# A fused attention and two-expert-layer kernel: one written order of all engines up to the third batch, and elementwise work moved off GpSimd

## Chip, cores and metric

One core of a Trainium2 chip. The metric is device time in microseconds (us), the median over runs of the same kernel. Engines are called TensorE (PE; its weight loads PEld), VectorE (DVE), ScalarE (ACT), GpSimd (POOL) and SyncE (SP), which issues most of the transfers.

## What is computed

Three layers follow each other. The inputs are arrays of 64-bit floats for the second layer's weights and of 32-bit floats elsewhere.

1. Attention on 4 batches of 8 heads, 768 positions, 64 wide. Each row sees the keys within 16 positions, and 24 summary keys: the maxima of K over blocks of 32 rows, with the means of V over the same blocks as their values.
2. A dense layer without a nonlinearity except a product, on 3072 rows: `a = x @ w1`, `b = x @ w2`, `x2 = ((a * b) @ w3) @ w_out`, with 512, 1024, 1024 and 512 columns.
3. A layer of 8 experts: rows whose score `x2 @ w_skip` is positive go to the expert with the largest of 8 logits, through `relu(x @ w1[e]) @ w2[e]`, scaled by the softmax weight and added to the row; other rows pass unchanged.

```python
k_sum = k.reshape(B, H, nb, block, D).max(axis=3)
v_sum = v.reshape(B, H, nb, block, D).mean(axis=3)
a = np.exp(scores_all)            # near keys and summaries, maximum subtracted
x = np.matmul(a / (np.sum(a, axis=-1, keepdims=True) + 1e-09), v_all)
h = (x @ w1) * (x @ w2) @ w3
x2 = h @ w_out
```

## The kernel before

**Two-part numbers.** The large products use a 32-bit format that TensorE takes at full rate, with each operand split in a high part and the remainder (the low part); a product is three matmuls, high by high, high by low and low by high. `split` (L410) does it: ScalarE copies the high part, VectorE (or an engine passed as `eng`) subtracts it.

**Narrowing.** The second layer's weights come as 64-bit floats, in 40 blocks of 128 by 512 (512 KB each). `Doubles.load` fetches a block to a raw tile, `scaled` makes two passes of ScalarE (L390, L391), and `narrow` three of VectorE: a clip (L400), the lower bits (L401), the sign (L404). Raw tiles come from a ring of 3 and 2 (`NRAW`, `XRAW`) while the fold runs, narrowed ones from a ring of 2 and 3 (`NNT`, `XNT`).

**Fold.** w3 and w_out are multiplied once into one matrix `wh`, `wl` (with the gate's columns in front: 522 columns in parts of 266 and 256), so that a row block needs a*b and one product `x2`.

**Attention** works on 16 pairs of heads (4 batches of 4). For a pair, K and Q are transposed (one PSUM tile, `tr`); then, for each third of the pair, letters name the steps: `S` the scores, `a` the masked minimum on VectorE (L196) and the exponential on ScalarE (L206), `b` the normalisation (L218 to L224), `T` and `t` the transposition and its copy, `V` and `v` the product with V and its copy. `m` loads half of the rows for the sums of V to the tile `vt`, of which there is one (`VTB = 1`), and `r` sums them (L134; with `pool` in four adds on GpSimd, L131 and L132). The loads of the next V tiles take the sums.

**Dense layer.** A row block is 256 rows; there are 12. Slabs (128 by 1024 in 32 bits; 7, then 12) hold attention's output, its two parts, and the two parts of each half of a*b. `ab` makes one of 8 chunks in 24 matmuls (L557), `ab_out` takes it from PSUM: a copy (L574), the product (L575), the high part (L576) and on GpSimd the low part (L577). `x2` makes the 96 matmuls of a block (L591) in 8 pieces of 12. The first four chunks of blocks 0 to 2 run as soon as half of w1 and w2 is there.

**Order.** Two strings (`PLAN`) give the order of the steps, a letter each, on all five engines, through the fold and the rest of the weights. After them only TensorE's order is written (`manual_schedule(engines={PE})`), by a generator (`AttentionOrder.plan`, `advance`) that puts attention steps between the pieces of the dense blocks; the other engines' instructions are placed by the framework. In the strings GpSimd has nine normalisations and three sums in the first, one of each in the second, and the low halves of the weights (14 in the first). The last batch's three blocks overlap with the splitting of the first expert's weights, and the experts run after them.

Of the kernel before, what the change touches and what calls it, by code (L numbers as in the profile page):

```python
# [7 lines left out]
F32 = mybir.dt.float32  # L8
# [52 lines left out]
STEPS = 11  # L61


class Attention:
# [60 lines left out]
    def sum(self, i, pool=False):  # L125
# [33 lines left out]
    def K_max(self, u):  # L159
        nc, f = self.nc, self.t.pop(("kn", "t"))  # L160
# [9 lines left out]
    def Q_out(self, u, act=False):  # L170
# [4 lines left out]
        if act:  # L175
# [40 lines left out]
    def S_norm(self, u, g, eng=None):  # L216
# [3 lines left out]
        if eng == "act":  # L220
            for i in range(4):
                nc.scalar.activation(pr[:, i, :], pr[:, i, :], AF.Copy, scale=st[:, 2, i : i + 1])
        else:
# [42 lines left out]
class AttentionOrder:  # L266


    KINDS = {
# [3 lines left out]
    }  # L273

    def __init__(self, att, pairs):
        self.att, self.pairs = att, pairs
        self.at = {c: 0 for c in self.KINDS}

    def step(self, c, eng=None):
        a, n = self.att, self.at[c]  # L280
        self.at[c] += 1
        if c == "k":
            a.load(n, "kn")
        elif c == "n":
            a.load(n, "qn")
        elif c == "w":
            a.load_v(n)
        elif c == "m":
            a.load_sum(n)
        elif c == "r":  # L290
            a.sum(n, eng == "pool")
        elif c == "j":
            a.Q_out(n, eng == "act")
        elif c in "KhHQ":
            {"K": a.K, "h": a.K_out, "H": a.K_max, "Q": a.Q}[c](n)
        elif c == "b":
            a.S_norm(*divmod(n, 3), eng)
        else:
            f = {"S": a.S, "a": a.S_exp, "T": a.T, "t": a.T_out, "V": a.V, "v": a.V_out}
            f[c](*divmod(n, 3))  # L300

    def upto(self, c, n):
        end = 4 * B if c in "mr" else self.pairs * self.KINDS[c]
        while self.at[c] < min(n, end):
            self.step(c)

    def plan(self):

        n, out = self.pairs, []
        out += [[("kKhH", 0)], [("nQj", 0)], [("kn", 1)]]  # L310
        for u in range(n):
            last = u + 1 == n
            head = [("kn", u + 2)] if u + 2 < n else []


            i = u + 4
            due = 8 <= i < 4 * B
            head += [("m", i)] if due else []
            out += [
                head + [("Sab", 3 * u)],  # L320
                [("Vv", 3 * u - 1)] if u else [],
                [("Sab", 3 * u + 1)],
                [("Tt", 3 * u)] + ([("r", i)] if due else []),
                [] if last else [("kK", u + 1)],
                [("Sab", 3 * u + 2)] + ([] if last else [("hH", u + 1), ("w", u + 1)]),
                [("Vv", 3 * u)],
                [] if last else [("nQj", u + 1)],
                [("Tt", 3 * u + 1)],
                [("Vv", 3 * u + 1)],
                [("Tt", 3 * u + 2)] + ([("Vv", 3 * u + 2)] if last else []),  # L330
            ]
        return out

    def run(self, todo):
        for cs, n in todo:
            for c in cs:
                self.upto(c, n + 1)
# [8 lines left out]
NRAW, XRAW = 3, 2  # L346
NS0, NS1 = 7, 12
NNT, XNT = 2, 3
WPOS = (6, 8, 9, 11, 12, 13, 14, 15)
PLAN = (  # L350
    (
        "fffAApOpfOAqskfomAssqRUAKuofpfUhsOfAHufpAoOUmpAspnAurffosOmUqQRocsuOAJXfUAopkpmuSUxsOuoS"
        "OaUKASfoabrUuXuznxXhwaATFfpFHFxetzAfFpXTQxfVeJtFXAvpFpAfASFaFpkXfxVfeAeSfXxvaspKFSTFzhna"
        "FHtzFTVXwfApQpffAekxtzevVfJpFnSxsFAvapTztfXFxeASwAappKVAFeSfXspfvAFTXxzkFFhaHptFexVAXzev"
        "fATtQJqfpTsFVFAwtvxpXdVTXxtfvFSFSeAAapxFfefsAzKaSaAmppFFeXVxFTshvRqteFXVxFvdFybeFe"
    ),
    (
        "fzABkpfATtBgsHgqVTBnvfByfmAsgtpBAgBVsfqgBffAsgvpByAgsqgAsfQBrgBABpgpmJngBrdsgSmRSK"
    ),
)  # L360


OTHER = {"z": ("b", "pool"), "Z": ("b", "act"), "R": ("r", "pool"), "J": ("j", "act")}


class Doubles:
# [29 lines left out]
    def narrow(self, raw, t):  # L396
        nc = self.nc
        h, l = raw[:, :, 1], raw[:, :, 0]
        tf = t.bitcast(F32)
        nc.vector.tensor_scalar(tf, tf, HIGH, -HIGH, ALU.min, ALU.max)  # L400
        nc.vector.scalar_tensor_tensor(  # L401
            out=t, in0=t, scalar=3, in1=l, op0=ALU.logical_shift_left, op1=ALU.bitwise_or
        )
        nc.vector.scalar_tensor_tensor(  # L404
            out=t, in0=h, scalar=-0x80000000, in1=t, op0=ALU.bitwise_and, op1=ALU.bitwise_or
        )
        return tf
# [115 lines left out]
class Dense:  # L523
    def __init__(self, tc, pool, slabs, halves, wh, wl, ps):
# [3 lines left out]
        self.xT, self.g = {}, {}  # L528
        self.spare = 2

    def has(self, b, k):
        return (b, k) in self.xT or len(self.slabs.free) > self.spare
# [33 lines left out]
    def ab_out(self, blk, f, pp):  # L566
        nc = self.nc
        if f % 4 == 0:
            if f:
                self.spare = 0  # L570
            self.g[blk, f // 4] = [self.slabs.take(F32R) for _ in range(2)]
        gh, gl = self.g[blk, f // 4]
        a = self.pool.tile([P, BT], F32, tag="a", name="a", bufs=2)
        nc.scalar.activation(a, pp[:, 0, :], AF.Copy)  # L574
        nc.vector.tensor_mul(a, a, pp[:, 1, :])  # L575
# [3 lines left out]
    def x2(self, blk, pool, out, x2e, route, finish):  # L579
        nc, i = self.nc, 2 * blk  # L580
        nf = FF // P
# [645 lines left out]
```

## Time and profile before

| what | value |
|---|---|
| median of 3 runs | 909.35 us (908.76 to 909.97) |
| the profiled execution's own time | 915.21 us |
| its span, first to last instruction | 913.3 us |
| mean granted TensorE clock | 0.968 |
| busy: PE, PEld, DVE, ACT, POOL | 830.8, 772.7, 478.9, 466.2, 223.9 us |
| moved by DMA | 105.02 MB |

Times count from the span's start. Matmuls are pipelined and their ends are modelled, so a busy TensorE need not be at its peak. The clock is granted at two levels, 1 (2.4 GHz) and 0.5; a stretch's value is the mean. In a view of stretches a row gives the stretch, its length, the busy time of PE, PEld, DVE, ACT and POOL with the number of instructions, the granted clock, the mean busy share of the 16 DMA engines and GB/s. In a view of lines a row gives line, engine, operation, output<-inputs, sizes and count, then busy us in all and mean ns of one, then the idle time of the engine just before them and what ended it. In a timeline a row gives start, duration, engine, line, operation, and in brackets the idle time before it with what ended it. L12 is line 12 of the kernel before.

### The profile page before, as it was taken

To read this page: it belongs to the slowest core of one execution; us is meant where nothing else is said; L and a number is where in the kernel's file an instruction comes from. 1 tells how busy PE (TensorE), PEld (TensorE's weight loads), DVE (VectorE), ACT (ScalarE), POOL (GpSimd) and SP (SyncE) were. 2 spreads that over 40 slices of the span, in tenths; PEclk is the share of its full clock that TensorE was granted. 3 is DMA by queue.
4 is the path that set the end of the run, shared out by engine and by line. 5 is a ranking of instruction groups with operands and counts; after the bars stand their busy time and mean duration, and the time that the engine had idled before them with its cause. 6 is when DMAs were issued, how large, how long until landed. Compare 5 with 4: busy or idle time off the path is not lost. (4 is left out here: it accounts for less than half of the span.)

```text
span 913.3 us, 17560 instructions
## 1 busy us (share of the span) xinstructions
PE 830.8 (91%) x6478; PEld 772.7 (85%) x6478; DVE 478.9 (52%) x1496; ACT 466.2 (51%) x1236; POOL 223.9 (25%) x278
## 2 busy tenths in 40 slices
PE   3779999968869999999999999999999979996996
PEld 3669888967769999999999999999998867874785
DVE  5869978845463545353535343522245466254862
ACT  5669986724435654544544544432244355243751
POOL 4312224531102121222121211222243112022231
PEclk9989999998898999999999999999999989997999
DMA  8587944442432433142232020421135456244830
GB/s 240 152 217 200 232 145 129 128 109 85 119 82 84 113 68 89 28 113 49 67 67 78 14 66 2 140 92 47 48 116 193 153 166 218 69 132 132 291 106 22
DMA packets 124612, 105.02 MB, mean 115 GB/s; under 512 B 92914, under 2 KB 98082, under 8 KB 124496
## 3 DMA queue, kind: packets, MB, share of 16 engines
q1 hardware_dynamic: 120144, 98.04, 37.5%
q0 software_dynamic: 4352, 5.51, 2.0%
q8 instruction: 64, 1.05, 0.5%
q14 instruction: 52, 0.43, 0.2%
HBM read 90.45 MB, written 16.64 MB: 117 GB/s over the span
## 5 line engine op out<-in xcount | busy, mean ns | idle before, releaser
L591 PE MATMUL x2p<-wh,slab 128*128 128x266 f32 (+1 forms) x768 | 158.7, 295 | 0.7 <-POOL slab L577 0.6
L591 PEld LDWEIGHTS x2p<-wh,slab 128*128 128x128 f32 x768 | 126.4, 193 | 2.4 <-POOL slab L577 1.0
L577 POOL TENSOR_TENSOR slab<-a,slab 128x256 fp32r<-128x256 f32 x96 | 73.8, 768 | 206.3 <-ACT slab L576 206.1
L591 PE MATMUL x2p<-wl,slab 128*128 128x256 f32 (+1 forms) x384 | 110.4, 287 | 0.0
L575 DVE TENSOR_TENSOR a<-a,ab 128x256 f32<-128x256 f32 x96 | 40.0, 417 | 123.8 <-ACT a L574 123.6
L206 ACT ACTIVATE pr<-pr,st 128x120 f32<-128x120 f32 x192 | 73.2, 384 | 50.2 <-DVE st L196 50.0
L574 ACT ACTIVATE a<-ab 128x256 f32<-128x256 f32 x96 | 36.5, 381 | 95.3 <-PE ab L557 94.1
L557 PE MATMUL ab<-slab,wB1h 128*128 128x256 f32 x384 | 75.6, 294 | 7.9 <-DVE a L575 6.1
L591 PEld LDWEIGHTS x2p<-wl,slab 128*128 128x128 f32 x384 | 74.5, 194 | 0.0
L557 PE MATMUL ab<-slab,wB2h 128*128 128x256 f32 x384 | 74.0, 291 | 0.0
L557 PE MATMUL ab<-slab,wA2h 128*128 128x256 f32 x384 | 72.0, 285 | 0.0
L557 PE MATMUL ab<-slab,wA1h 128*128 128x256 f32 x384 | 72.0, 285 | 0.0
L557 PEld LDWEIGHTS ab<-slab,wB1h 128*128 128x128 f32 x384 | 61.3, 197 | 9.1 <-DVE a L575 6.6
L576 ACT ACTIVATE slab<-a 128x256 fp32r<-128x256 f32 x96 | 40.0, 417 | 55.2 <-DVE a L575 55.0
L557 PEld LDWEIGHTS ab<-slab,wB2h 128*128 128x128 f32 x384 | 60.5, 194 | 0.5
L196 DVE CUSTOM_DVE_ANT_0 pr<-sp,cst 128x120 f32<-128x120 f32 x192 | 42.5, 277 | 34.3 <-PE sp L184 33.3
L557 PEld LDWEIGHTS ab<-slab,wA1h 128*128 128x128 f32 x384 | 58.9, 189 | 0.3
L557 PEld LDWEIGHTS ab<-slab,wA2h 128*128 128x128 f32 x384 | 58.9, 189 | 0.1
L877 POOL DMA_INDIRECT out<-eo,idx x15 | 19.5, 1299 | 149.9 <-DVE eo L874 96.8
L557 PE MATMUL ab<-slab,wB1l 128*128 128x256 f32 x192 | 55.3, 288 | 0.0
L184 PE MATMUL sp<-kaug,qblk 128*128 128x120 f32 x384 | 51.6, 278 | 3.4 <-DVE st L196 3.4
L557 PE MATMUL ab<-slab,wB2l 128*128 128x256 f32 x192 | 54.5, 284 | 0.0
(182 smaller groups left out, 2184.7 us busy)
## 6 DMA issues: line engine op xcount, KB each, us to landing
eraw<-in_moe_w SPq DMA_DIRECT2D x64, 512.0 KB, 5.1
raw<-in_moe_w SPq DMA_DIRECT2D x32, 512.0 KB, 5.2
vaug<-in_v SPq DMA_DIRECT2D x32, 240.0 KB, 5.4
x2e<-row SPq DMA_DIRECT2D x24, 256.5 KB, 2.9
kn<-in_k SPq DMA_DIRECT2D x32, 192.0 KB, 3.1
vt<-in_v SPq DMA_DIRECT2D x16, 384.0 KB
qn<-in_q SPq DMA_DIRECT2D x32, 192.0 KB, 3.0
out<-row SPq DMA_DIRECT2D x24, 256.0 KB
```

The costliest lines, as they stand in the source:

```text
L184: self.nc.tensor.matmul(sp[:, i, 0:KA], self.qblk[:, t, :, :], self.kaug[:, t, :], start=True, stop=True)
L196: nc.vector.tensor_tensor_reduce(out=pr[:, i, :], in0=sp[:, i, 0:KA], in1=self.cst[:, m : m + KA], scale=1.0, scalar=3.0e38, op0=ALU.add, ...
L206: nc.scalar.activation(pr[:, i, :], pr[:, i, :], AF.Exp, scale=-1.0, bias=st[:, 0, i : i + 1], accum_out=st[:, 1, i : i + 1],)
L557: self.nc.tensor.matmul(pp[:, s, :], l[:, c, fs], r[:, c, :], start=(c == 0 and j == 0), stop=(c == 3 and j == 2),)
L574: nc.scalar.activation(a, pp[:, 0, :], AF.Copy)
L575: nc.vector.tensor_mul(a, a, pp[:, 1, :])
L576: nc.scalar.activation(gh[:, f % 4, :], a, AF.Copy)
L577: nc.gpsimd.tensor_sub(gl[:, f % 4, :], a, gh[:, f % 4, :].bitcast(F32))
L591: nc.tensor.matmul(po[:, 0:n], l[:, f % 4, s * P : s * P + P], r[:, f, lo:hi], start=(f == 0 and j == 0), stop=(f == nf - 1 and j == 2),)
L877: nc.gpsimd.indirect_dma_start(out=self.out, out_offset=bass.IndirectOffsetOnAxis(ap=col, axis=0), in_=o, in_offset=None, bounds_check=N - ...
```

## The change

One written order of all five engines now goes on to the end of the third batch's blocks: three strings take the place of two strings and the generator, with new letters for pieces of `x2` (`E`), its copies (`G`) and the router's second part (`N`). Narrowing is three steps with letters of their own (`p`, `i`, `d`). The sums, normalisations and low halves that GpSimd had go to VectorE; the sum is four adds there and no longer a reduction. For blocks 0 to 2 the first half of a*b is kept as one slab and split later (`gsplit`, letter `l`). Raw tiles are 3 and 1 while the fold runs, narrowed tiles 2 and 1; slabs 8, then 12. For the first 8 pairs both halves of Q are copied by ScalarE.

```diff
-NRAW, XRAW = 3, 2
-NS0, NS1 = 7, 12
-NNT, XNT = 2, 3
-WPOS = (6, 8, 9, 11, 12, 13, 14, 15)
+NRAW, XRAW = 3, 1
+NNT, XNT = 2, 1
+NS0, NS1 = 8, 12
+HALVES = 3
+JOBS = "oooooooottttttttwttwttwttwttwwwwwwwwwwww"
...
-        if pool:
-            for n in (8, 4, 2):
-                nc.gpsimd.tensor_add(vt[:, 0:n, :], vt[:, 0:n, :], vt[:, n : 2 * n, :])
-            nc.gpsimd.tensor_add(sm, vt[:, 0, :], vt[:, 1, :])
-        else:
-            nc.vector.tensor_reduce(
-                out=sm, in_=vt.rearrange("r j d -> r d j"), axis=AX.X, op=ALU.add
-            )
+        for n in (8, 4, 2):
+            nc.vector.tensor_add(vt[:, 0:n, :], vt[:, 0:n, :], vt[:, n : 2 * n, :])
+        nc.vector.tensor_add(sm, vt[:, 0, :], vt[:, 1, :])
...
-            (nc.gpsimd if eng == "pool" else nc.vector).tensor_mul(
-                pr, pr, st[:, 2, :].unsqueeze(2).to_broadcast([P, 4, KA])
-            )
+        nc.vector.tensor_mul(pr, pr, st[:, 2, :].unsqueeze(2).to_broadcast([P, 4, KA]))
...
-    def narrow(self, raw, t):
+    def clip(self, t):
...
+    def lower(self, raw, t):
...
+    def signed(self, raw, t):
...
-def split(nc, hi, lo, src, eng=None):
+def split(nc, hi, lo, src):
     nc.scalar.activation(hi, src, AF.Copy)
-    (eng or nc.vector).tensor_sub(lo, src, hi.bitcast(F32))
+    nc.vector.tensor_sub(lo, src, hi.bitcast(F32))
...
+    def ab_out(self, blk, f, pp, whole=False):
+        nc, h = self.nc, f // 4
         a = self.pool.tile([P, BT], F32, tag="a", name="a", bufs=2)
         nc.scalar.activation(a, pp[:, 0, :], AF.Copy)
+        if whole:
+            if f % 4 == 0:
+                self.whole[blk, h] = self.slabs.take(F32)
+            nc.vector.tensor_mul(self.whole[blk, h][:, f % 4, :], a, pp[:, 1, :])
+            return
...
         nc.scalar.activation(gh[:, f % 4, :], a, AF.Copy)
-        nc.gpsimd.tensor_sub(gl[:, f % 4, :], a, gh[:, f % 4, :].bitcast(F32))
+        nc.vector.tensor_sub(gl[:, f % 4, :], a, gh[:, f % 4, :].bitcast(F32))
+
+    def gsplit(self, blk, h):
+        self.g[blk, h] = [self.slabs.take(F32R) for _ in range(2)]
+        w = self.whole.pop((blk, h))
+        split(self.nc, *self.g[blk, h], w)
+        self.slabs.give(w)
...
             nar_s.close()
             att.more = nar_s.enter_context(sb("more", "right"))
+            for c in PLAN[2]:
+                op(c)
             order.__exit__(None, None, None)
             order = tc.manual_schedule(engines={PE})
             order.__enter__()
```

The three strings have 428, 174 and 507 letters. The third begins as follows (`B` a chunk of a*b, `g` its way out of PSUM, `k`, `n`, `w` the loads of K, Q and V, `y` the split of a block of attention's output):

```
hgBHEQgyTEatBjmEVvnbTBGrgtSKVgvaBTEkSgtwbBVaGbETvlSEtnaVETEgHvNGtEVhQGEvbjTkSyEbBgBBgBgmGrtmBEgE
...
```

`K_max` still copies K's maxima on GpSimd (L165), and the router its running counts (L656).

## Rows read from the trace of the kernel before

**Rows 1.** Busy time of each engine by stage, and in the first stage's densest part.

```profile
8.00:144.50 136.50, 110.94 (x896) 103.26 (x895) 112.12 (x264) 105.01 (x273) 37.65 (x39) 0.95 0.76 197
...
184.00:280.00 96.00, 73.76 (x587) 70.41 (x586) 49.06 (x195) 36.19 (x125) 17.97 (x29) 0.88 0.37 100
280.00:587.00 307.00, 305.39 (x2859) 298.37 (x2858) 134.73 (x661) 151.90 (x493) 60.68 (x88) 1.00 0.25 64
...
90.00:105.00 15.00, 13.61 (x125) 13.01 (x124) 14.44 (x37) 13.83 (x38) 3.73 (x3) 1.00 0.97 239
```

**Rows 2.** Timeline of TensorE, 184 to 280 us: the four longest holes.

```profile
197.31 0.80 PE L557 MATMUL ab<-slab,wB1h 128*128 128x256 f32 x2 [5.33 <-DVE a L575]
...
218.52 1.54 PE L147 MATMUL tr<-ident,qn 128*128 128x128 f32 x6 [3.79 <-DVE ks L162]
...
243.81 1.18 PE L184 MATMUL sp<-kaug,qblk 128*128 128x120 f32 x8 [2.79 <-DVE st L196]
...
273.49 1.11 PE L232 MATMUL tp<-ident,pr 128*120 128x128 f32 x4 [6.13 <-DVE st L196]
```

**Rows 3.** Timeline of VectorE, in two of these holes.

```profile
241.09 1.86 DVE L134 TENSOR_REDUCE sm<-vt 96x64 f32<-96x1024 f32 x1 [4.35 <-DMA vt<-in_v]
...
270.70 1.86 DVE L134 TENSOR_REDUCE sm<-vt 96x64 f32<-96x1024 f32 x1 [3.72 <-DMA vt<-in_v]
```

**Rows 4.** Waits of VectorE, 184 to 280 us: us in total, times, longest us.

```profile
DVE sm L134 <- DMA vt<-in_v: 22.7, 7, 4.4
```

**Rows 5.** Timeline of SyncE: issues of the loads for the sums.

```profile
233.62 0.67 SPq L122 DMA_DIRECT2D vt<-in_v  x1
...
255.11 9.15 SPq L122 DMA_DIRECT2D vt<-in_v  x2
```

**Rows 6.** Lines of VectorE, 8 to 144.5 us.

```profile
L401 DVE SCALAR_TENSOR_TENSOR nt<-nt,raw 128x512 int32<-128x512 int32 x31 | 27.5, 888 | 2.1
L404 DVE SCALAR_TENSOR_TENSOR nt<-raw,nt 128x512 int32<-128x512 int32 x31 | 25.6, 824 | 1.1
L400 DVE TENSOR_SCALAR nt<-nt 128x512 f32<-128x512 f32 x30 | 16.2, 540 | 1.0 <-ACT nt L390 1.0
L412 DVE TENSOR_TENSOR tl<-w3t,th 128x512 fp32r<-128x512 f32 x16 | 10.9, 682 | 6.4 <-ACT th L411 6.3
...
L134 DVE TENSOR_REDUCE sm<-vt 96x64 f32<-96x1024 f32 x2 | 3.7, 1865 | 5.4 <-DMA vt<-in_v 5.4
```

**Rows 7.** Lines of VectorE and GpSimd, the whole span.

```profile
L577 POOL TENSOR_TENSOR slab<-a,slab 128x256 fp32r<-128x256 f32 x96 | 73.8, 768 | 206.3 <-ACT slab L576 206.1
...
L575 DVE TENSOR_TENSOR a<-a,ab 128x256 f32<-128x256 f32 x96 | 40.0, 417 | 123.8 <-ACT a L574 123.6
...
L224 DVE TENSOR_TENSOR pr<-pr,st 128x480 f32<-128x480 f32 x38 | 27.1, 713 | 0.4
...
L412 DVE TENSOR_TENSOR slab<-slab,slab 128x1024 fp32r<-128x1024 f32 x15 | 18.3, 1222 | 8.6 <-ACT slab L411 6.2 <-PE ab L557 1.6 <-PE x2p L591 0.7
```

**Rows 8.** The narrowed tile `nt`: ns min/median/max of VectorE's three steps.

```profile
L400 DVE TENSOR_SCALAR nt<-nt x40: 395/421/1322, 5.6 to 178.5; 128x512 f32<-128x512 f32 x40
L401 DVE SCALAR_TENSOR_TENSOR nt<-nt,raw x40: 691/693/2289, 6.2 to 178.9; 128x512 int32<-128x512 int32 x40
L404 DVE SCALAR_TENSOR_TENSOR nt<-raw,nt x40: 691/692/1775, 6.9 to 179.7; 128x512 int32<-128x512 int32 x40
```

**Rows 9.** Timelines of VectorE and of GpSimd at the same moment.

```profile
88.66 1.21 DVE L400 TENSOR_SCALAR nt<-nt 128x512 f32<-128x512 f32 x1
...
88.60 0.99 POOL L224 TENSOR_TENSOR pr<-pr,st 128x480 f32<-128x480 f32 x1 [4.53 <-DVE st L219]
```

**Rows 10.** Timelines of ScalarE and TensorE: one narrowed block's first write, last read.

```profile
73.94 0.67 ACT L390 ACTIVATE nt<-raw 128x512 f32<-128x512 f32 x1
...
92.62 0.60 PE L433 MATMUL w3t<-ident,nt 128*128 128x128 f32 x4
```

**Rows 11.** Timeline of TensorE at the end of the third batch.

```profile
584.79 0.69 PE L246 MATMUL ov<-pt,vaug 120*64 120x64 f32 x16 [1.19 <-ACT pt L238]
```

More of the change, by code (lines that the diff above doesn't have):

```diff
@@ L302, in upto @@
[L302 to L337, printed above, removed]
+    KINDS = "knwmrKhHQjSabTtVv"
+    def __init__(self, att):
+        self.at = {c: 0 for c in self.KINDS}
+        one = {
+            "k": lambda n: att.load(n, "kn"), "n": lambda n: att.load(n, "qn"),
+            "w": att.load_v, "m": att.load_sum, "r": att.sum,
+            "K": att.K, "h": att.K_out, "H": att.K_max, "Q": att.Q, "j": att.Q_out,
+        }
+        three = {
+            "S": att.S, "a": att.S_exp, "b": att.S_norm,
+            "T": att.T, "t": att.T_out, "V": att.V, "v": att.V_out,
+        }
+        self.f = dict(one)
+        for c, g in three.items():
+            self.f[c] = lambda n, g=g: g(*divmod(n, 3))
@@ L340, with step @@
+    def step(self, c):
+        n = self.at[c]
+        self.at[c] += 1
+        self.f[c](n)
 VTB = 1
@@ L527, in __init__ @@
         self.wh, self.wl = wh, wl
[L528 to L532, printed above, removed]
+        self.xT, self.g, self.whole = {}, {}, {}
+        self.po, self.rows, self.wide = {}, {}, None
     def get_xT(self, b, k):
@@ new lines, in ab_out, with x2 @@
+        nc.vector.tensor_sub(gl[:, f % 4, :], a, gh[:, f % 4, :].bitcast(F32))
+    def gsplit(self, blk, h):
+        self.g[blk, h] = [self.slabs.take(F32R) for _ in range(2)]
+        w = self.whole.pop((blk, h))
+        split(self.nc, *self.g[blk, h], w)
+        self.slabs.give(w)
+    def x2(self, n):
+        blk, q = divmod(n, 8)
+        half, s, h = q // 4, q // 2 % 2, q % 2
+        lo, hi = ((0, WSPLIT), (WSPLIT, WX))[half]
+        if h == 0:
+            self.po[n // 2] = self.ps.tile([P, 512], F32, tag="x2", name="x2p", bufs=2)
+        po = self.po[n // 2]
+        gh, gl = self.g[blk, h]
+        for f in range(4):
+            for j, (l, r) in enumerate(((gh, self.wh), (gh, self.wl), (gl, self.wh))):
+                self.nc.tensor.matmul(
+                    po[:, 0 : hi - lo],
+                    l[:, f, s * P : s * P + P],
+                    r[:, 4 * h + f, lo:hi],
+                    start=(h == 0 and f == 0 and j == 0),
+                    stop=(h == 1 and f == 3 and j == 2),
+                )
@@ new lines, in x2_out @@
+    def x2_out(self, n, out, x2e, route):
+        nc, pool, po = self.nc, self.wide, self.po.pop(n)
+        blk, q = divmod(n, 4)
+        half, s = divmod(q, 2)
+        i = 2 * blk + s
+        lo, hi = ((0, WSPLIT), (WSPLIT, WX))[half]
+        if half == 0:
+            self.rows[i] = row = pool.tile([P, XE], F32, tag="row", name="row", bufs=2)
+            lg = pool.tile([P, 10], F32, tag="lg", name="lg", bufs=2)
+            nc.vector.tensor_copy(lg, po[:, 0:10])
+            nc.scalar.activation(row[:, 0 : hi - 10], po[:, 10:hi], AF.Copy)
+            route(i, row, lg)
+        else:
+            row = self.rows.pop(i)
+            nc.scalar.activation(row[:, lo - 10 : DM], po[:, 0 : hi - lo], AF.Copy)
+            rs = slice(i * P, (i + 1) * P)
+            nc.sync.dma_start(out=x2e[rs, :], in_=row)
+            nc.sync.dma_start(out=out[rs, :], in_=row[:, 0:DM])
+            if s:
+                for h in range(2):
+                    self.drop(self.g.pop((blk, h)))
@@ L1069, in fused, with load, scaled, signed @@
-            route, finish, counts, start = router(tc, rp, cst, tok, idx, idxd, ps)
+            route, finish, counts, start = router(tc, rp, cst, tok, idx, idxd, ps)
+            def load(n):
+                raws[n] = dbl.load(source(jobs[n]))
+            def scaled(n):
+                ready[n] = dbl.scaled(raws[n])
+            def signed(n):
+                ready[jobs[n]] = dbl.signed(raws.pop(n), ready[n])
+            def wsplit(n):
+                j = splits[n]
+                if j[0] == "o":
+                    hi, lo = fold.oh[:, j[1], 10:WX], fold.ol[:, j[1], 10:WX]
+                else:
+                    hi, lo = (t[:, j[3], :] for t in halves[j[1]][j[2]])
+                split(nc, hi, lo, ready[j])
@@ L1070, in fused @@
+            at = {c: 0 for c in steps}
+            def op(c):
+                if c in ao.f:
+                    ao.step(c)
+                else:
+                    at[c] += 1
+                    steps[c](at[c] - 1)
             for c in PLAN[0]:
```

305 lines of the change are left out of this document (100 added, 205 removed), and 3 rows, old and new, of the table KINDS.

## The prediction

> **What bounds the kernel now.** I read the busy times by stage first [rows 1], then, for the stage that stood out, TensorE's instructions with the idle time ahead of them [rows 2], then what the engine named there had itself been waiting for [rows 3 to 5]. TensorE is the bound in most of the run: from 280 to 587 us (the third stage below) it is busy 305.39 of 307 us at the full clock, and there the change can win nothing. Two stages are different. In the first (8 to 144.5 us: narrowing the weights, the fold of w3 and w_out, the first batch's attention) TensorE is busy 110.94 of 136.5 us while VectorE is busy 112.12 and ScalarE 105.01, and the DMA engines are at 0.76; in its densest part VectorE is busy 14.44 of 15 us and the DMA share is 0.97. No single engine holds this stage; VectorE and the transfers are close to it. The second is 184 to 280 us: no engine is full (TensorE 73.76, VectorE 49.06, ScalarE 36.19 of 96 us), the DMA share is 0.37, and the granted clock is 0.88. A stage in which nothing is full waits for an order.
>
> The waits are four holes of 2.79 to 6.13 us, each ended by VectorE [rows 2]. In two of them VectorE stood idle for 4.35 and 3.72 us ahead of the reduction of `vt` (the sums of V, L134) [rows 3], and seven such waits for the load of `vt` are 22.7 us in this stage [rows 4]. The queue shows why [rows 3, 5]: each load goes out when the one buffer falls free, and the reduction, next in VectorE's queue, starts about 7 us later (233.62 plus 0.67 to 241.09; the second of two issues, ending at 264.26, to 270.70). All that stands behind it on VectorE (softmax, a*b products) waits too, and with it TensorE. After each hole the matmuls run at the lower clock for a while.
>
> **What the second stage holds.** Idle 96 - 73.76 = 22.2 us. A mean clock of 0.88 out of the levels 1 and 0.5 (2.4 and 1.2 GHz) means 0.24 of 96 us, 23 us, at the lower level, where half of the work is lost: 11.5 us. Together 33.7 us, against an equal stretch of the third stage [rows 1].
>
> **The change, part by part.**
>
> (1) *The sums of V.* Eight of the sixteen load-and-sum pairs now stand in the first string, two in the second, six in the third. For the last eight I counted the matmuls that the strings put between load and sum and took 0.107 us each (307 us over 2859 [rows 1]): 17.8, 14.3, 6.0, 0, 6.8, 6.8, 97.6 and 0 us. The two zeros look bad, but SyncE need not wait for TensorE: there the buffer has been free for 39.2 and 15.8 us of matmul work, so the load goes out as soon as the queue ahead of it has been issued. Only the thirteenth has its buffer freed by the sum just before, 6.8 us against the 7 us of a load. I take the holes as closed: -33.7 us. Bounds: 0 (every sum still waits) to -33.7.
>
> (2) *GpSimd's work moves to VectorE, in the first stage.* Fourteen low halves of weights: 14 x 0.682 = 9.5 us [rows 6]; nine normalisations: 9 x 0.713 = 6.4 us [rows 7]; three sums that GpSimd made and three that came later before. A sum is now four adds of 512 to 64 elements; VectorE has none in this trace, but the reduction that they replace takes 1.865 us, so six cost up to 11.2 us; I take 9.6 us (1.6 us each, estimated from 0.682 for 512 elements and 0.417 for 256, less for the rest). In all 25.5 us. Against it stands what VectorE gets back. Its narrowing steps take 0.421, 0.693 and 0.692 us at the median [rows 8] but 0.540, 0.888 and 0.824 us on average in this stage [rows 6], and a long one is to be seen: 1.21 us for the first step, begun while GpSimd normalises from 88.60 to 89.59 us [rows 9]. Thirty-one times 0.12, 0.20 and 0.13 is 14 us. Net, VectorE gets 11.5 us more on 112.
>
> Here the Trainium skill speaks against the change: the page "Perfetto Trace Analysis", section "Optimizing Scalar/DVE Operations", says that work may be handed to GpSimd when VectorE is saturated. By that, with nothing given back, VectorE's work in the stage would be 137.6 us and not 123.6. The same passage adds that the two share a port, so that handing over might not help; with that the trace agrees (1.21 us against a median of 0.421 [rows 8, 9]).
>
> At VectorE's present share of the stage (112.12 / 136.5 = 0.82) 123.6 us take 151 us, at the 0.96 of the densest part 129 us, each plus 8 us of start. Today the stage ends at 144.5 us; with about 3.9 us of matmuls that the first string adds (one a*b chunk, a transposition, a product with V: 44, of which 16 are small) the mark is 148.4. So between 10 us later and 12 us earlier; I take +2 us, since the buffers shrink too: raw blocks go from five to four and narrowed ones from five to three in this stage. One life of a narrowed block went from 73.94 to 93.22 us [rows 10], and 31 blocks in 136.5 us are 4.4 us each, so that three buffers suffice only while a life is under 13.2 us on average.
>
> (3) *The low half of a*b, 96 times.* GpSimd's subtraction takes 0.768 us; on VectorE I take 0.417, as its product of the same size [rows 7]. Some 84 of them and three whole slabs of 1.222 us are 39 us of VectorE work after 144.5 us, where it is at most about half busy from 184 us on. On ScalarE twelve quarter copies go and three of whole slabs come. Cover: matmuls. I count 0; without the cover a chunk would cost its 0.4 us.
>
> (4) *One order for all engines to 587 us.* In each queue a late instruction now holds all behind it: an unfinished transposition keeps ScalarE from the next product, and a row that isn't written keeps SyncE from the next K and V. This trace doesn't show the cost, since after the second string only TensorE's order was fixed. From below it is the 1.6 us of idle time in the third stage; from above as much as the present holes, 33.7. The strings leave at least 0.8 us of other matmuls between a transposition and its use, mostly several us, so I stay near the lower end: one hole like that of 2.79 us, plus a quarter of the 11.5 us lost at the lower clock, 5.7 us.
>
> (5) *The seam.* The next block's split (1.222 us on VectorE, behind about as much on ScalarE [rows 7]) now comes behind the strings' last step on both queues, and TensorE, out of work, waits: about 2.5 us, besides the 1.19 us of today [rows 11], which I leave as it is. What follows has the same matmuls in the same order: 0.
>
> **Sum.** The profiled execution took 915.21 us (span 913.3). -33.7 + 2 + 0 + 5.7 + 2.5 = -23.5, which gives 891.7. It stood 5.9 us above the median of 909.35, so on the scale of the runs shown I forecast 886.
>
> **Rivals.** *The first stage shortens as well* (0.22): VectorE, no longer held up by GpSimd, reaches the share of its densest part and the stage ends 12 us ahead of the mark, not 2 behind it: 872 us. For it: the inflated means [rows 6]. Against it: the transfers at 0.97 in that part.
>
> *New holes eat half* (0.18): the fixed queues stall somewhere else, a further 17 us: 903 us. For it: five of eight load-to-sum distances are under the 7 us of a load. Against it: the free buffer.
>
> *Slower: three narrowed blocks are too few* (0.14). If a block's life stays at 16 us, between the 13.2 that three buffers allow and the 19.3 of the one shown [rows 10], a block takes 16 / 3 = 5.3 us, 32 of them 171 us, and with 8 us of start the first stage ends at 179, 31 us behind the mark. Less the 2 that I put there: 886 + 29 = 915 us. It decides from a mean life of 13.2 us on. For it: the length of that one, and low halves that now wait in VectorE's queue. Against it: VectorE makes a low half in 0.682 us [rows 6], where GpSimd takes 0.768 for half the size [rows 7].
>
> That the change doesn't do what it says is no case of its own, but it is not wholly true: the copy of K's maxima and the router's small additions stay on GpSimd.
>
> **How the numbers follow.** The likeliest case has 0.46, its own range 877 to 896. No case lands on 909; the upper edge of the second rival gives 0.04 to the band of 0.2% around it (about what a measurement of this kernel can tell from no change). Faster: 0.46 + 0.22 + 0.14 = 0.82; same 0.04; slower 0.14. The range from 861 to 909 leaves out the slower case and a thin tail below.
>
> **What would show it.** Right: no wait of VectorE for `vt` over 2 us after 184 us; TensorE over 95% busy from there to the seam, at clock 1.00; narrowing steps near their medians; the fold's last matmul near 150 us. Wrong: a fold that ends after 165 us, with ScalarE's scaling step waiting for a narrowed block's buffer; or holes that have only moved, to waits of TensorE for ScalarE.

## The result, and the profile after

The changed kernel takes **878.0 us** (median of 4 runs, 876.47 to 879.82) against 909.5 us (908.76 to 909.97) for the kernel before beside it: ratio 0.9655, 95% interval 0.9634 to 0.9677. The forecast was 886, range 861 to 909.

| profiled execution | before | after | difference | forecast |
|---|---|---|---|---|
| start to the fold's last matmul | 144.5 | 140.9 | -3.6 (-7.5 against the mark of 148.4) | +2 |
| from there to the seam (block 8's last `x2` matmul) | 442.6 | 409.5 | -33.1 (-29.2 at equal work) | -25.5 |
| seam to the end | 326.2 | 325.0 | -1.2 | 0 |
| span | 913.3 | 875.4 | -37.9 | -23.5 |

The forecast of the second row is terms (1), (4) and (5) together. The medians differ by 31.5 us and the spans by 37.9: the profiled execution of before stood some 6 us above its median, that of after (877.20 us) 0.8 below its own. Little of it lies ahead of the fold's end, since runs 1, 2 and 5, with the same first string, end the fold at 143.7 to 145.1 us; behind the seam runs 2, 3 and 5, with the same work, take 323.3 to 325.3 us against 326.2. So a few of the 6 us may stand in the second row, whose -33.1 is then that much too large; one profiled execution can't settle it.

First the stages of the changed kernel; the columns are those of [rows 1].

```profile
8.00:140.90 132.90, 114.23 (x901) 108.34 (x902) 110.19 (x307) 103.65 (x262) 2.46 (x4) 0.97 0.79 202
184.00:280.00 96.00, 95.26 (x881) 93.30 (x880) 52.34 (x222) 54.87 (x165) 6.39 (x11) 1.00 0.39 91
280.00:550.00 270.00, 267.25 (x2488) 260.82 (x2487) 151.16 (x659) 127.55 (x426) 17.68 (x33) 1.00 0.28 68
```

From 184 to 280 us TensorE is busy 95.26 of 96 us, not 73.76, at a granted clock of 1.00, not 0.88. The price in the third stage is small: 2.75 us idle in 270. VectorE's busy time from 280 to 550 us went from 119.76 to 151.16 us, and of the waits listed first below 1.7 us are TensorE's waits for VectorE in that stretch.

Next, all waits of TensorE from 144.5 us to the seam, and VectorE's waits for `vt` from 184 us to the seam (us in total, times, longest).

```profile
PE sp L178 <- ACT pt L226: 1.0, 1, 1.0
PE tp L220 <- DVE pr L214: 0.8, 2, 0.6
PE sp L178 <- DVE qblk L172: 0.7, 1, 0.7
PE ab L504 <- DVE slab L362: 0.5, 1, 0.5
PE tp L220 <- DVE slab L251: 0.4, 1, 0.4
```

```profile
DVE vt L129 <- DMA vt<-in_v: 2.0, 1, 2.0
```

The four holes of [rows 2] and the seven stands of [rows 4] are gone. What is left is 3.4 us in six small holes, and one stand of 2.0 us. A stand is a time in which VectorE is idle because the next instruction of its queue waits for a load or for another engine.

VectorE's narrowing steps (ns min, median, max, as in [rows 8]) and its normalisations, low halves and sums up to the fold's end (as in [rows 6]):

```profile
L346 DVE TENSOR_SCALAR nt<-nt x40: 411/420/645, 5.8 to 178.8; 128x512 f32<-128x512 f32 x40
L349 DVE SCALAR_TENSOR_TENSOR nt<-nt,raw x40: 673/683/911, 6.3 to 179.3; 128x512 int32<-128x512 int32 x40
L354 DVE SCALAR_TENSOR_TENSOR nt<-raw,nt x40: 674/682/694, 7.1 to 180.5; 128x512 int32<-128x512 int32 x40
```

```profile
L214 DVE TENSOR_TENSOR pr<-pr,st 128x480 f32<-128x480 f32 x11 | 7.2, 657 | 0.4
L362 DVE TENSOR_TENSOR ol<-nt,oh 128x512 fp32r<-128x512 f32 x8 | 5.5, 684 | 0.5 <-ACT oh L361 0.3
L129 DVE TENSOR_TENSOR vt<-vt 96x512 f32<-96x512 f32 x7 | 4.8, 684 | 7.6 <-DMA vt<-in_v 7.6
...
L129 DVE TENSOR_TENSOR vt<-vt 96x256 f32<-96x256 f32 x7 | 2.9, 421 | 0.2
...
L129 DVE TENSOR_TENSOR vt<-vt 96x128 f32<-96x128 f32 x7 | 2.0, 288 | 0.2
...
L212 DVE TENSOR_SCALAR st<-st 128x4 f32<-128x4 f32 x11 | 1.8, 160 | 0.0
L130 DVE TENSOR_TENSOR sm<-vt 96x64 f32<-96x64 f32 x7 | 1.5, 221 | 0.2
```

Almost no step is stretched any more: the longest clip takes 645 ns, where it took 1322. That one and the longest second step (911 ns) overlap GpSimd's copies of K's maxima, which stayed there (28.56 to 29.28 and 109.89 to 110.38 us). A sum's four adds are 684 + 421 + 288 + 221 = 1614 ns (the forecast had 1.6 us).

### The profile page after: what moved, and what is told of

Its sections match the earlier page's. It is cut to its first block, busy times and chain, and to the rows that moved or that the text cites. A ratio compares the mean times of both kernels' runs of the same rounds, so it can differ in the third digit from the quotient of the medians.

```text
span 875.4 us, 17512 instructions
## 1 busy us (share of the span) xinstructions
PE 821.2 (94%) x6478; PEld 766.4 (88%) x6478; DVE 513.4 (59%) x1663; ACT 466.0 (53%) x1230; POOL 99.3 (11%) x135
## 5 line engine op out<-in xcount | busy, mean ns | idle before, releaser
L547 PE MATMUL x2p<-wh,slab 128*128 128x266 f32 (+1 forms) x768 | 156.1, 290 | 0.0
L526 DVE TENSOR_TENSOR a<-a,ab 128x256 f32<-128x256 f32 x84 | 35.2, 419 | 76.5 <-ACT a L517 76.0
L504 PE MATMUL ab<-slab,wB1h 128*128 128x256 f32 x384 | 72.5, 287 | 0.0
L504 PE MATMUL ab<-slab,wB2h 128*128 128x256 f32 x384 | 70.7, 282 | 0.0
L527 ACT ACTIVATE slab<-a 128x256 fp32r<-128x256 f32 x84 | 35.0, 417 | 63.6 <-DVE a L526 63.1
L504 PEld LDWEIGHTS ab<-slab,wB1h 128*128 128x128 f32 x384 | 58.9, 190 | 0.4
L528 DVE TENSOR_TENSOR slab<-a,slab 128x256 fp32r<-128x256 f32 x84 | 36.1, 430 | 38.7 <-ACT slab L527 38.2
L786 ACT ACTIVATE hr<-hp 128x512 f32<-128x512 f32 x30 | 17.9, 598 | 71.1 <-PE hp L782 71.0
L504 PE MATMUL ab<-slab,wA2l 128*128 128x256 f32 x192 | 54.1, 282 | 0.0
L504 PE MATMUL ab<-slab,wA1l 128*128 128x256 f32 x192 | 54.1, 282 | 0.0
```

The costliest lines, as they stand in the source:

```text
L504: self.nc.tensor.matmul(pp[:, s, :], l[:, c, fs], r[:, c, :], start=(c == 0 and j == 0), stop=(c == 3 and j == 2),)
L528: nc.vector.tensor_sub(gl[:, f % 4, :], a, gh[:, f % 4, :].bitcast(F32))
L547: self.nc.tensor.matmul(po[:, 0 : hi - lo], l[:, f, s * P : s * P + P], r[:, 4 * h + f, lo:hi], start=(h == 0 and f == 0 and j == 0), stop ...
L786: nc.scalar.activation(hr, hps[s], AF.Relu)
```

## The experiments

The kernels below change either the kernel before or the changed one. Fold's end and seam are those of the profiled execution, in us; ratios are to the kernel before on the same chip, measured beside each run.

| run | from | median | ratio (95%) | fold's end | seam |
|---|---|---|---|---|---|
| before | | 909.5 | 1 | 144.5 | 587.1 |
| after | | 878.0 | 0.9655 (0.9634 to 0.9677) | 140.9 | 550.4 |
| 1, no late sums | before | 873.9 | 0.9621 (0.9600 to 0.9643) | 143.7 | 563.0 |
| 2, VectorE ordered | before | 927.6 | 1.0188 (1.0162 to 1.0214) | 144.9 | 603.8 |
| 3, nothing on GpSimd | before | 918.0 | 1.0107 (1.0082 to 1.0132) | 147.3 | 590.9 |
| 4, third string on TensorE alone | after | 875.9 | 0.9638 (0.9617 to 0.9658) | 142.9 | 550.1 |
| 5, second buffer for sums | before | 901.0 | 0.9890 (0.9869 to 0.9911) | 145.1 | 577.6 |
| 6, weights and normalisation on GpSimd | after | 880.9 | 0.9669 (0.9646 to 0.9693) | 142.3 | 552.2 |
| 7, low halves of a*b on GpSimd | after | 880.6 | 0.9675 (0.9652 to 0.9698) | 141.3 | 550.8 |
| 8, four narrowed blocks | after | 877.7 | 0.9627 (0.9599 to 0.9655) | 140.4 | 550.0 |
| 9, sums crowded | after | 896.4 | 0.9858 (0.9821 to 0.9896) | 139.1 | 563.0 |
| 10, first string on TensorE alone | after | 871.9 | 0.9576 (0.9540 to 0.9612) | 135.2 | 545.0 |
| 11, sum as a reduction | after | 882.6 | 0.9695 (0.9656 to 0.9734) | 142.9 | 553.5 |
| 12, runs 4 and 8 together | after | 874.2 | 0.9608 (0.9575 to 0.9640) | 138.1 | 545.9 |

The fold's end has a spread of its own: with the same first string it came at 138.1 to 142.9 us (after and runs 4, 7, 8, 9, 12; those of 8 and 12 had one more buffer). Differences of 2 us there say nothing.

### 1. Before, without the late sums

```diff
-        src = self.vs[p * NBLK : (p + 1) * NBLK, b, :, :]
+        src = self.vs[p * NBLK : (p + 1) * NBLK, b % 2, :, :]
...
-            due = 8 <= i < 4 * B
+            due = False
```

The loads and sums of V for the last two batches are left out; these batches take the sums of the first two.

> The kernel before without the loads and sums of V for the last two batches (they take the first two batches' sums, so that part of the computation is left out). Theory: the holes of 184 to 280 us come from VectorE standing at these eight sums; without them the stage loses nearly all its idle time and its low clock, and the time falls by 25 to 34 us, to 876 to 885. Rival: the holes come from the free order of the other engines as such, and VectorE would stand at the next late thing; then the time falls by under 10 us.

The seam comes 24.1 us earlier, 23.3 of them behind the fold's end. The rest of this run's gain lies behind the seam (308.7 us against 326.2), where other values send rows to other experts, and isn't used. Stage 184 to 280 us, then TensorE's two long waits in it:

```profile
184.00:280.00 96.00, 88.92 (x815) 86.19 (x816) 43.35 (x228) 51.21 (x174) 21.51 (x34) 0.96 0.37 89
```

```profile
PE ab L557 <- DVE a L575: 4.9, 1, 4.9
PE ab L557 <- DVE slab L412: 1.7, 1, 1.7
```

By the forecast's own rule 96 - 88.92 = 7.1 us of idle time and half of 0.08 x 96 us at the lower clock, 3.8, are left: 10.9 of the 33.7 us, so 22.8 should have gone, and 23.3 did. The rule that priced the stage holds, but only about two thirds of the 33.7 us hang on the late sums; the rest hangs on another wait. VectorE's timeline shows which, in this run, and the list of its waits from 184 to 280 us shows the same one in the kernel before:

```profile
193.42 0.22 DVE L139 TENSOR_TENSOR sm<-sm 96x64 f32<-96x64 f32 x1 [5.75 <-POOL sm L132]
```

```profile
DVE sm L139 <- POOL sm L132: 6.2, 1, 6.2
```

VectorE adds two half sums and stands 5.75 us for the one that GpSimd makes, still in the second string. It is not one of the forecast's seven stands, and the change takes it away too. In the kernel before it stands ahead of the hole of 5.33 us, the first of [rows 2], so that one was not made by a load of `vt`.

### 2. Before, with VectorE's order fixed

```diff
-            order = tc.manual_schedule(engines={PE})
+            order = tc.manual_schedule(engines={PE, ET.DVE})
```

It holds from the second string's end to the third batch's end.

> The kernel before, with VectorE's order fixed as well as TensorE's after the second string, up to the third batch's end; nothing else changes. Theory: the framework had moved the eight sums ahead of their place in the text; with VectorE in written order each load goes out long before its sum, VectorE's waits for vt in 184 to 280 us fall from 22.7 us to under 5, and the time falls by 15 to 30 us. Rival: the written order of the generator was never meant for VectorE, other instructions then stand at its head, and the time rises or stays within 5 us.

Slower by 1.6 to 2.1%. VectorE no longer waits for `vt` after 184 us, but TensorE does no better (its waits in 184 to 280 us, then the longest in its timeline):

```profile
PE ab L557 <- DVE slab L412: 18.8, 2, 12.7
```

```profile
197.40 0.58 PE L557 MATMUL ab<-slab,wB1h 128*128 128x256 f32 x1 [12.71 <-DVE slab L412]
```

TensorE is busy 74.94 of 96 us at clock 0.89, as before, and from 280 to 550 us it now falls to 256.98 of 270. The generator's list was written for TensorE; read as an order for VectorE it holds a new block's low half (195.94 us) behind what isn't ready, here the sum that GpSimd makes (VectorE waits 5.87 us for it, to 194.52). In the kernel before the same low half ran at 184.82 us, ahead of that sum. Here, then, an order as such closed nothing; it has to be laid out for the engine that it binds.

### 3. Before, with nothing on GpSimd

The normalisations, sums and low halves that GpSimd had go to VectorE, letters in the same places:

```diff
-        nc.gpsimd.tensor_sub(gl[:, f % 4, :], a, gh[:, f % 4, :].bitcast(F32))
+        nc.vector.tensor_sub(gl[:, f % 4, :], a, gh[:, f % 4, :].bitcast(F32))
```

> The kernel before, with all that GpSimd did for normalisations, sums, and low halves on VectorE (sums as one reduction), in the old order. Prediction's account: the narrowing steps fall to their medians (0.42, 0.69, 0.69 us), VectorE has 10 us more work in the first stage, which ends between 142 and 152 us; the holes behind the sums stay; in all between -6 and +8 us. Rival: taking GpSimd away is itself a main part of the gain; then -10 us or more.

It costs 8 us, just outside the expected -6 to +8. The fold ends 2.8 us later, and the second stage keeps its stands (`DVE sm L134 <- DMA vt<-in_v: 24.6, 8, 5.0`). The spans of the two profiled executions differ by 2.9 us only, since that of before was some 6 us slow; where the other 5 us of the medians stand isn't shown. The narrowing steps confirm what GpSimd did to them; to 147.3 us they take their medians:

```profile
L401 DVE SCALAR_TENSOR_TENSOR nt<-nt,raw 128x512 int32<-128x512 int32 x31 | 21.7, 700 | 1.9 <-ACT raw L391 0.2
L404 DVE SCALAR_TENSOR_TENSOR nt<-raw,nt 128x512 int32<-128x512 int32 x31 | 21.5, 693 | 1.1
L400 DVE TENSOR_SCALAR nt<-nt 128x512 f32<-128x512 f32 x30 | 12.6, 419 | 0.1
```

That is 55.8 us against 69.3 in [rows 6]: 13.5 us back, where the forecast had 14.

### 4. After, with the third string on TensorE alone

```diff
-            for c in PLAN[2]:
-                op(c)
             order.__exit__(None, None, None)
             order = tc.manual_schedule(engines={PE})
             order.__enter__()
+            for c in PLAN[2]:
+                op(c)
```

> The changed kernel with the third string fixing TensorE's order alone, as before; the other engines are placed by the framework. Theory: its six sums are moved ahead and VectorE stands at them again: five or six holes, 15 to 25 us slower than the changed kernel (893 to 903), early in the third string. Rival: the strings' contents (pieces of x2, whole halves) carry the gain, not the order of the other engines; then within 5 us of 878.

That expectation failed: 875.9 us, no slower. The framework pulls the last six sums forward, all to before 280 us as in the kernel before, and VectorE stands again:

```profile
DVE vt L129 <- DMA vt<-in_v: 7.8, 4, 3.4
```

TensorE has one hole of 1.6 us there. The longest two stands show why none came of them (VectorE's timeline):

```profile
239.60 0.42 DVE L526 TENSOR_TENSOR a<-a,ab 128x256 f32<-128x256 f32 x1
243.06 0.69 DVE L129 TENSOR_TENSOR vt<-vt 96x512 f32<-96x512 f32 x1 [3.05 <-DMA vt<-in_v]
...
259.70 0.42 DVE L528 TENSOR_TENSOR slab<-a,slab 128x256 fp32r<-128x256 f32 x1
263.48 1.14 DVE L129 TENSOR_TENSOR vt<-vt 96x512 f32<-96x512 f32 x2 [3.36 <-DMA vt<-in_v]
```

Each comes just behind the product or the low half of a chunk of a*b, and TensorE is inside a piece of `x2` or the next chunk until the stand is over. So a written order for the other four engines in the third string is not what closed the second stage; which part of TensorE's new order is (the pieces of `x2`, the whole halves, the places of the sums) wasn't taken apart.

### 5. Before, with a second buffer for the sums

```diff
-        vt = self.pool.tile([4 * NBLK, 16, D], F32, tag="vt", name="vt", bufs=VTB)
+        pool = self.more if self.more and i % 2 else self.pool
+        vt = pool.tile([4 * NBLK, 16, D], F32, tag="vt", name="vt", bufs=VTB)
```

> The kernel before with a second buffer for the rows of V's sums once the fold is over; order and amount of work stay. Theory: it is VectorE's waits on the one buffer that make the holes; with two, a load goes out while the sum before it is still waiting, the seven waits (22.7 us) fall under 10 us, the holes at 215, 241 and 267 us shrink or go, and the time falls by 15 to 24 us (885 to 895). Rival: the transfers themselves are late (SyncE's queue), or TensorE's tight order makes the holes whatever VectorE waits for; then the time falls by under 5 us.

Between the two: 9 us by the medians. In the profiled executions the seam comes 9.5 us earlier, and what follows it is 2.9 us shorter. The stands shrink from 22.7 to 12.7 us, and some still reach TensorE, whose longest wait in the stage is 5.0 us for a product. The one buffer is worth about a third of the gain; this run doesn't show what the rest is.

### 6 to 8. After, with one part taken back

Run 6 gives GpSimd the 16 low halves of the first weights and nine normalisations, eight of them ahead of the fold's end:

```diff
-                split(nc, hi, lo, ready[j])
+                split(nc, hi, lo, ready[j], nc.gpsimd if n < 16 else None)
```

> The changed kernel with the low halves of the first sixteen weight blocks and the normalisations of the first batch (from the fourth on) back on GpSimd, at the same places in the order. Prediction's account: VectorE loses 13 us of own work and gets longer narrowing steps back (about 10 us), so the first stage ends within 4 us of 140.9 and the time within 4 us of 878. Rival: the contention was the larger part; then 5 to 15 us slower, with narrowing steps of 0.8 to 0.9 us on average.

Run 7 gives it the low halves of a*b:

```diff
-        nc.vector.tensor_sub(gl[:, f % 4, :], a, gh[:, f % 4, :].bitcast(F32))
+        nc.gpsimd.tensor_sub(gl[:, f % 4, :], a, gh[:, f % 4, :].bitcast(F32))
```

> The changed kernel with the low half of a*b back on GpSimd (84 subtractions in the dense blocks). Prediction's account: under cover either way, within 2 us of 878. Rival: GpSimd's 0.77 us, and what it takes from VectorE, reach TensorE through the pieces of x2; then 3 to 8 us slower.

Run 8 gives narrowed blocks a fourth buffer:

```diff
-NNT, XNT = 2, 1
+NNT, XNT = 2, 2
```

> The changed kernel with four buffers for narrowed blocks instead of three while the fold runs; order the same. Prediction's third rival: if three bind, ScalarE's first scaling pass starts earlier, the first stage ends 3 to 10 us before 140.9 and the time falls as much. Theory: a life stays under 13.2 us on average and three do; then within 2 us of 878.

All three intervals overlap that of the changed kernel. In run 6 the longest narrowing steps are 1507, 1758 and 1796 ns again, and some 16 us of work taken off VectorE lower its busy time to the fold's end by 3.2 us only (106.99 against 110.19). By the medians moving GpSimd's work is worth 3 us here, either part, but the overlap leaves room for nothing. Run 7's 2.6 us lie between its two expectations. A fourth buffer changed nothing that could be measured.

### 9. After, with the late sums crowded

Each of the last eight sums stands directly behind its load; TensorE's order and all queues stay. In the strings `m` becomes `mr`, and the later `r` goes:

```diff
-        "hgBHEQgyTEatBjmEVvnbTBGrgtSKVgva...
+        "hgBHEQgyTEatBjmrEVvnbTBGgtSKVgva...
```

> The changed kernel with each of its last eight sums of V moved directly behind the load that it sums, in strings two and three; TensorE's order stays as it is, and all five engines keep their written order. Theory (the distance between load and sum is what closed the second stage's holes): VectorE now stands up to 7 us at most of these eight sums, some 30 to 45 us in all, TensorE shows holes of 2 to 6 us at several of them again, and the time rises by 12 to 30 us, to 890 to 908. Rival (new strings keep enough of TensorE's work between a product and its use, so that such waits of VectorE no longer reach it, as the run with only TensorE's order in the third string suggests): VectorE waits as long, but TensorE's holes in 184 to 280 us stay under 4 us in sum and the time within 5 us of 878.

The loss has the theory's size, but neither its place nor its stands: VectorE stands at three sums only, 14.7 us in all where 30 to 45 were expected, all after 280 us. In order, its stands in 280 to 550 us, the stage, and TensorE's longest wait there:

```profile
DVE vt L129 <- DMA vt<-in_v: 14.7, 3, 7.0
```

```profile
280.00:550.00 270.00, 258.84 (x2352) 252.72 (x2350) 142.09 (x618) 119.11 (x397) 17.48 (x32) 0.98 0.28 68
```

```profile
PE ab L504 <- DVE a L526: 9.7, 3, 3.6
```

9.7 us of holes, and half of 0.04 x 270 us at the lower clock, 5.4, are 15.1; from the fold's end to the seam the kernel takes 423.9 us, 14.4 more than the changed one. (The profiled execution took 891.88 us, 4.5 below the run's median, so the loss of 18 us by the medians isn't seen whole.) Here the stand comes in front of the product (VectorE's timeline, then TensorE's, with the last matmuls of the two chunks before):

```profile
288.05 1.46 DVE L129 TENSOR_TENSOR vt<-vt 96x512 f32<-96x512 f32 x3 [4.58 <-DMA vt<-in_v]
...
289.69 0.41 DVE L526 TENSOR_TENSOR a<-a,ab 128x256 f32<-128x256 f32 x1
```

```profile
280.10 0.28 PE L504 MATMUL ab<-slab,wA2l 128*128 128x256 f32 x1
...
282.95 0.28 PE L504 MATMUL ab<-slab,wB2l 128*128 128x256 f32 x1
...
290.16 0.51 PE L504 MATMUL ab<-slab,wB1h 128*128 128x256 f32 x2 [3.40 <-DVE a L526]
```

Chunks of a*b have two PSUM buffers (`bufs=2` in `ab`), and the next chunk needs the one of the chunk two before it. Both held finished chunks: one since 280.38 us, whose product (289.69 to 290.10) the stand held up, and one since 283.23. TensorE starts the next chunk 0.06 us after that product, and just so at the other two holes (309.46 to 309.52, 326.64 to 326.70). The stands of 4.58, 3.12 and 7.02 us left holes of 3.40, 2.71 and 3.59. Beside run 4, where stands of 3.05 and 3.36 us cost nothing, this is the point: not how long VectorE stands, but whether TensorE's next step needs a product that is behind it. In run 4 the next chunk after either stand found its buffer free for 6.5 us or more.

### 10 to 12. The first string, the form of the sum, and a combination

Run 10 fixes the first string for TensorE alone:

```diff
-            order = tc.manual_schedule(engines=ENGINES)
+            order = tc.manual_schedule(engines={PE})
...
+            order.__exit__(None, None, None)
+            order = tc.manual_schedule(engines=ENGINES)
+            order.__enter__()
             fold_s.close()
```

> The changed kernel with its first string fixed for TensorE alone; the other engines' instructions of that string are placed by the framework, strings two and three stay as they are. The changed kernel's fold ends at 140.9 us, though moving GpSimd's work to VectorE without a new order had put it at 147.3 instead of 144.5. Theory (the written order of all engines in the first string is what the first stage gained by): the fold ends at 148 to 156 us and the time is 884 to 893. Rival (the order of TensorE in the new first string, with less of the attention held back, is enough): the fold ends within 3 us of 140.9 and the time within 4 us of 878.

Both expectations miss: it is faster than the changed kernel, the two intervals apart. The fold ends at 135.2 us, below all six of the spread above, and the whole gain is there: the seam comes 5.4 us earlier too. From 45 us to the fold's end, first VectorE's longest wait and TensorE's in the changed kernel, then TensorE's in this one:

```profile
DVE wl L362 <- ACT wh L361: 4.4, 3, 2.7
...
PE po L428 <- DVE wl L362: 4.6, 4, 2.6
...
PE ov L234 <- ACT pt L226: 2.6, 1, 2.6
```

```profile
PE po L428 <- DVE wl L362: 2.5, 1, 2.5
PE sp L178 <- issue: 2.2, 2, 1.4
PE sp L178 <- ACT pt L226: 1.3, 1, 1.3
```

In the written order VectorE stands at the low half of the fold's product until ScalarE has made the high half, and TensorE's fold waits for it; left free, VectorE waits 0.2 us there. But this wait of TensorE's shrank by 2.1 us only, of 4.1 us of idle time that went in all (12.1 to 8.1). Another that went is ScalarE's wait for raw blocks (8 us to the fold's end, the changed kernel, then this one):

```profile
ACT nt L338 <- DMA raw<-in_moe_w: 9.6, 4, 3.9
```

```profile
ACT nt L338 <- DMA raw<-in_moe_w: 2.4, 1, 2.4
```

Which of the four freed engines brings the gain wasn't taken apart.

Run 11 makes the sum one reduction:

```diff
-        for n in (8, 4, 2):
-            nc.vector.tensor_add(vt[:, 0:n, :], vt[:, 0:n, :], vt[:, n : 2 * n, :])
-        nc.vector.tensor_add(sm, vt[:, 0, :], vt[:, 1, :])
+        nc.vector.tensor_reduce(
+            out=sm, in_=vt.rearrange("r j d -> r d j"), axis=AX.X, op=ALU.add
+        )
```

> The changed kernel with each sum of V made by one reduction on VectorE instead of four adds. The reduction took 1.865 us before; the four adds, by the trace of the changed kernel, some 1.5 us together. Theory (the price in the first stage's sum, 1.6 us for six sums, was about right and the form hardly matters): the fold's end and the time stay within 2 us of 140.9 and 878. Rival (VectorE is close enough to the bound in the first stage that eight times 0.3 us and the longer single instruction show): the fold ends 2 to 5 us later and the time is 880 to 883.

Inconclusive: 882.6 us lies in the rival's 880 to 883, but the intervals overlap, and the fold's end of 142.9 us is that of run 4 as well.

Run 12 joins runs 4 and 8.

> The two variants that came out level with or just below the changed kernel together: third string fixed for TensorE alone, and four buffers for narrowed blocks instead of three. If their small leads (875.9 and 877.7 against 878.0) are real and add up, the time is 873 to 876 and the ratio about 0.962; if they are the spread of the measurement, 877 to 880.

874.2 us fits the first reading, but its interval still touches that of the changed kernel (0.9640 against 0.9634). Run 10 is the fastest version found, 871.9 us. Runs 4 and 10 together were not run.

## Why the prediction was right, and where its steps were not

The direction, the second stage and its cause held; the gain in the first stage was not forecast. Step by step:

**(1) The sums of V, -33.7.** Right in place and about in size. The second part of the run lost 29.2 us at equal work; with 3.4 us of new holes, which belong to (4), that is some 32.6, or a few us less if the slow profiled execution of before lost its time there. Run 1 shows that 23 of it hang on the late sums. Most of the rest stands beside a wait of the same kind, for a sum that GpSimd made; no run took that one away alone. The counted distances held as well: the one sum whose buffer was freed 6.8 us ahead, the thirteenth, is the one that stands in the changed kernel (2.0 us, at 291.9). Where my reading was too short is the chain from stand to hole: I had every stand cost TensorE time. Runs 4 and 9 show that a stand costs when TensorE's next step needs what is behind it, in run 9 the product that frees one of two full chunk buffers (in [rows 2] mostly a step of the attention), and is free when it doesn't. Run 2 shows that removing the stands with an order made for another engine brings nothing.

**(2) GpSimd's work, +11.5 us on VectorE and +2 at the fold's end.** This term was mis-sized: the fold ended 7.5 us before the mark, not 2 behind it. VectorE was busy 110.19 us to the fold's end, where 123.6 were forecast. The parts that I priced were good (1614 ns for a sum, 684 for a low half, 13.5 us back on narrowing), but I gave back too little: of two normalisations that VectorE already had one took 2.91 us beside GpSimd, where one now takes 0.657, and its 11 additions on 128x4, 356 ns on average before, take 160. Also, only seven sums stand ahead of the fold's end, and one step of the attention fewer. All durations on VectorE in the stage add up to 128.5 us against 125.4, but consecutive instructions overlap in the records, more so after, and the busy time fell by 1.9. The share did not move: 110.19 of 132.9 us is 0.83, and with the 0.82 that I used, the right work gives 8 + 110.19 / 0.82 = 142.4 us. The price of the move alone is about what I took: run 3 puts the fold's end 2.8 us later in the old order (2.2 to 3.6 beside runs 1, 2 and 5). The other 10 us came with the new first string. What in it brings them (TensorE's order, the ring of raw blocks, Q's copies on ScalarE) wasn't taken apart. That the other four engines are bound there is not it: by run 10 this costs 5 to 6 us.

The Trainium skill, in "Perfetto Trace Analysis", section "Optimizing GPSIMD Operations", says to prefer other engines to GpSimd where possible. By that alone run 3 should have won; it lost 8 us, so the trace doesn't agree for the old order, and in the new one (runs 6 and 7) the two differ by less than 3 us. The skill's "SBUF — State Buffer", section "Who interferes with whom", says that a VectorE instruction with two inputs in SBUF contends with a GpSimd instruction that reads SBUF, and one with a single input only in the modes that use both ports. The stretched normalisation and two-input narrowing steps agree (2.91 us for 0.657, up to 2.289 for 0.693); the clip and the addition in the last section have one input, and no row shows in which mode they ran.

**(3) Low halves of a*b, 0.** Right: run 7 differs by less than the measurement can tell. The low half takes 430 ns on VectorE (84 of them, 36.1 us), and 761 on GpSimd.

**(4) One order for all engines, +5.7.** Right in sign and somewhat high for the part after the fold: the holes there sum to 3.4 us, with no lower clock. What I did not price is the first string, since the kernel before had such an order there too: run 10 puts the cost at 5 to 6 us.

**(5) The seam, +2.5.** Too high. The next block's first chunk starts at 551.0 without a hole, and the last one ahead of it is 0.63 us, where there was one of 1.19.

**The rivals.** The first stage did shorten, by 7.5 us against the mark where that rival had 12, so the truth lies between the likeliest case and it; its reason, VectorE freed from GpSimd, is not shown to be it: run 3 takes GpSimd out of VectorE's way in the old order and the fold ends later, and run 6, which gives much of the work back, ends it within the spread. New holes did not come. Three narrowed blocks were not too few: ScalarE's scaling step waits 1.4 us for a block that TensorE still reads and 3.9 for one that VectorE does, and a fourth buffer changed nothing. The signs that I named came out: no stand over 2.0 us, TensorE over 95% busy at clock 1.00, narrowing at its medians; only the fold's end was forecast too late.

## What to carry to other kernels

An idle stage in which no engine is full can be priced by its idle time and lower clock; here an experiment that deletes part of the awaited work took away, without any reordering, what that rule gave for the part (22.8 us by the rule, 23.3 measured). A stand of an elementwise engine for a transfer was free where TensorE's next buffers had been released before it, and cost half to nine tenths of its length where that release was queued behind it: place the awaited step right behind the release. Write an order only for the engine that needs one; here TensorE's was enough in the third string, in the first better by 6 us than one for five engines (the second was never freed), and an order made for TensorE made things worse when VectorE was bound to it.

## What the runs showed of the hardware

The lower clock goes with some holes of a few us: in run 9 the holes of 3.40 and 3.59 us were each followed by a stretch at 1.2 GHz (3.4 us from 291.3 on, 6.8 us from 325.4 on), the hole of 2.71 us by none. The stage's granted clock is 0.98 for it instead of 1.00, some 5 us lost beside 9.7 of idle time. In the kernel before the hole of 2.79 us [rows 2] was followed by one of 6.8 us. Behind the fold's end the changed kernel's holes of 1.0 us and less left the clock at 1.00.

GpSimd stretches more on VectorE than the long steps, and in the rows below for as long as its own instruction lasts. In the kernel before (timelines of VectorE and of GpSimd):

```profile
79.18 1.26 DVE L218 TENSOR_SCALAR st<-st 128x4 f32<-128x4 f32 x1
```

```profile
79.12 1.30 POOL L412 TENSOR_TENSOR wA1l<-nt,wA1h 128x512 fp32r<-128x512 f32 x1 [14.62 <-ACT wA1h L411]
```

An addition on four elements per partition, 0.16 us in the changed kernel, begins 0.06 us after GpSimd's subtraction and ends 0.02 us after it (80.44 against 80.42).
